# A planner that knows of a shared port: new costs, margins and priorities, and a first batch in chunks of 1, 1, 2 and 2 token tiles

## The chip, the cores and the metric

One core of one Trainium2 chip. The metric is the device time of one execution in microseconds (us), from outside the program; the profile's span is the time from the first to the last instruction of one profiled execution, and is a little shorter.

## The reference

```python
scores = scale * np.matmul(q, k.transpose(0, 1, 3, 2))      # q, k, v: 4 x 8 x 768 x 64
...
scores = np.where(mask, scores, -1000000000.0)
scores = scores - np.max(scores, axis=-1, keepdims=True)
attn = np.exp(scores)
attn = attn / (np.sum(attn, axis=-1, keepdims=True) + 1e-09)
x = np.matmul(attn, v)          # as 3072 x 512: tokens by heads and dims
h = x @ w_in                    # 512 x 2048
g = np.maximum(h, 0.0) + alpha * np.minimum(h, 0.0)
out = g @ w_out                 # 2048 x 512
```

The mask has blocks of 32 tokens: neighbours, the first and last rows and columns, and three drawn blocks for each row. All 768 x 768 scores are computed. The weights arrive as float64.

## The kernel before

Precision: each float32 operand is split into a large float16 part and a small float16 remainder, and a product is three float16 matmuls (large by large, and the two cross terms). So every operand has, besides its own work, a step `hi` (scale and round, line 322 on) and a step `lo` (scale, subtract, lines 330 to 336). On VectorE (DVE) `lo` is one instruction, on GpSimd (POOL) two: a one-input scale (line 335) and a two-input subtraction (line 336). The float64 weights are first made float32 with integer steps on the bits, called n1, n2 and n3 (lines 708, 713 or 715, and 720).

Tiling: a token tile is 128 tokens. A batch has 768 tokens and was cut in three chunks of two tiles (`SIZES0`, and `[2, 2, 2]` for the others). A unit is one chunk and one pair of heads; a step is one token tile of one head, 192 steps in all. This text calls blocks of TensorE (PE) matmuls:
- S block (line 498): the scores of one step, 128 x 768, four matmuls. Then DVE adds the mask and takes the row's extreme (`e`, line 508), ScalarE (ACT) does the exponential (line 515), DVE the reciprocal `rs` (line 523), and P is written as its large part (`ph`, DVE line 327 or ACT line 325) and small part (DVE line 333 or POOL lines 335 and 336). SyncE (SP) transposes P by DMA (line 538).
- A block (line 552): attention times v for one unit, 36 matmuls of 256 columns. Its result `x` is split on ACT and DVE (lines 563 and 568).
- U block (line 852): x by a 256-wide piece of w_in, 24 matmuls of 256 columns, eight for a chunk. Then the activation block on DVE (`g`, lines 862 and 863), the large part `gh` on ACT (line 868) and the small part `gl` on POOL (line 873).
- D block (line 891): g by w_out, 12 matmuls of 512 columns.

U needs x of the chunk's four units and the split w_in; D needs gh, gl and the split w_out. K's scales of all four head pairs of a batch go into `cs`, which every `e` of a later chunk needs; K loads (`kf`) and V loads use the buffers `vf`.

Order: nothing is left to the hardware. The class `Plan` is a list scheduler: each operation has a priority (smaller is earlier; attention step n has about n), costs for the engines that may do it, the operations that it waits for, and buffers to take and free. `run` walks through a model of time, picks an engine for each ready operation, and gives the order in which the kernel is then written; at the end every engine's instructions are chained in that order. Priorities of the weights' steps come from `V_WI`, `W_WI`, `V_WO` and `W_WO`, those of U and D from `MOE_LAG`, and `MOE_BOOST` puts the steps behind U ahead. A cost written as a pair was, for DVE, the time alone and the time while POOL is busy.

Of the kernel before, what the change touches and what calls it, by code (L numbers as in the profile page):

```python
# [23 lines left out]
PSCALE = 2.0**14  # L24
GSCALE = 2.0**-20
SB = 205 << 23
SIZES0 = [2, 2, 2]
MOE_LAG = 11.753
MOE_BOOST = 7.325
V_WI = -10.661  # L30
W_WI = 1.102
V_WO = 12.217
W_WO = 1.038
WI_LO = "pe"
PL_V = -12.594
P_V = -6.546
PL = "ggv"
LD = 4


class Buf:
# [13 lines left out]
class Plan:  # L55
# [2 lines left out]

    ENGINES = ("PE", "DVE", "ACT", "POOL", "SP")
    SHARE = {"SP": 0.3, "ACT": 0.7}  # L60
    LAT = {"PE": 0.15, "DVE": 0.11, "ACT": 0.12, "POOL": 0.08}

    def __init__(self, pools):
        self.ops, self.free = [], dict(pools)
# [11 lines left out]
    def run(self):  # L76
# [31 lines left out]

        def cost(o, e):
            c = o.alts[e]  # L110
            if isinstance(c, tuple):
                c = c[1] if idle["POOL"] > now + 0.2 else c[0]
            return c

        while left:
            progress = True
            while progress:
                progress = False
                ready.sort(key=lambda o: (o.prio, o.n))
                load = dict.fromkeys(self.ENGINES, 0.0)  # L120
                taken = []
                for o in ready:
                    if any(not b.live and self.free[b.pool] <= 0 for b in o.alloc):
                        continue
                    best = min(o.alts, key=lambda e: max(idle[e] - now, 0.0) + load[e] + cost(o, e))
                    if idle[best] > now + 1e-9 or load[best] > 0:
                        load[best] += cost(o, best)
                        continue
                    c = cost(o, best)
                    o.eng, o.start = best, now  # L130
# [12 lines left out]
                    progress = True  # L143
                for o in taken:
                    ready.remove(o)
            both = all(rings.values())
            heads = [(r, self.SHARE[x] if both else 1.0) for x, r in rings.items() if r]
            t_dma = min((now + r[0][0] / w for r, w in heads), default=None)
            t_ev = min((e[0] for e in events), default=None)
            assert t_dma is not None or t_ev is not None, [  # L150
                (o.n, o.prio, o.alts, [(b.pool, self.free[b.pool]) for b in o.alloc]) for o in ready[:12]
            ]
            nxt = min(t for t in (t_dma, t_ev) if t is not None)
            for r, w in heads:
                r[0][0] -= (nxt - now) * w
            now = nxt
            for r, _ in heads:
                if r[0][0] <= 1e-9:
                    events.append((now + 0.9, r[0][1].n, "fin", r[0][1]))
                    r.pop(0)  # L160
            due = sorted(e for e in events if e[0] <= now + 1e-9)
            events = [e for e in events if e[0] > now + 1e-9]
            for _, _, kind, o in due:
                if kind == "dma":
                    rings["SP" if o.eng == "SP" else "ACT"].append([o.dma, o])
                elif kind == "fin":
                    finish(o)
        self.span, self.busy = now, busy
# [4 lines left out]
def attn_moe(ctx: ExitStack, tc: tile.TileContext, q, k, v, sampled, w_in, w_out, alpha, out):  # L173
# [9 lines left out]
    NC = DM // P  # L183
    W2 = 2 * P

    bufs = dict(kt=5, ks=5, v2=5, vf=5, qf=6, qt=3, qn=2, ph=4, e=3, pt=3, x=2, g=3, gh=3, gl=3, junk=2, sid=2)
# [150 lines left out]

    T = {}
    LQ = {"ACT": 0.06}
    MAX4 = {"DVE": (0.55, 1.1), "ACT": 0.85}  # L340
    LOW4 = {"DVE": (0.94, 1.5), "POOL": 2.8}


    steps = [(u, j) for u, (c, hp) in enumerate(units) for j in range(2 * chunks[c][2])]
# [264 lines left out]
    def prep_q(c, prio, pl, gate):  # L609
# [16 lines left out]
        for u, fb in zip(us, fbs):  # L626
            hp = units[u][1]
            p = prio if c == 0 else first[u] - 5
            nb = plan.buf("qn")
            o = plan.op(p, {"POOL": 0.35 + 0.25 * f, "ACT": 0.15 + 0.25 * f, "DVE": (0.1 + 0.15 * f, 0.2 + 0.4 * f)},  # L630
                        lambda e, u=u: emit_q_hi(e, u), [sc[hp]], [nb], [fb])
            o = plan.op(p, {"DVE": (0.14 + 0.27 * f, 0.2 + 0.65 * f)}, lambda u=u: emit_q_lo(u), [o], [], [nb, fb])
            qtbuf[u] = plan.buf("qt")
            o_qt[u] = plan.op(p - 2, {"SP": 0.8 * f}, lambda u=u: emit_q_t(u), [o], [qtbuf[u]], [nb], dma=0.75 * f)

    def attend(n):
# [9 lines left out]
        o = plan.op(n - 2, {"ACT": 0.11}, lambda: emit_dn(n), [o])  # L646
        o = plan.op(n - 2, {"DVE": 0.08}, lambda: emit_rs(n), [o])
        o = plan.op(n - 1, MAX4, lambda e: emit_p_hi(e, n), [o], [pb], [eb])
        lo = {"POOL": 2.8} if PL[n % len(PL)] == "g" else {"DVE": (0.94, 1.5)} if PL[n % len(PL)] == "v" else LOW4
# [6 lines left out]
    def values(u):  # L656
# [8 lines left out]
        o = plan.op(p - 2, {"PE": 0.4 + 1.92 * f}, lambda: emit_av(u), last + [o_v2[b, hp]],  # L665
                    [ab, xbuf[c]], [ptbuf[u, 0], ptbuf[u, 1], vbuf[b, hp]])
        o = plan.op(p - 4, {"ACT": 0.1 + 0.2 * f}, lambda: emit_x_hi(u), [o], [], [ab, xbuf[c]])
        o_x[u] = plan.op(p - 4, {"DVE": 0.1 + 0.25 * f}, lambda: emit_x_lo(u), [o], [], [ab, xbuf[c]])
# [128 lines left out]
    for f in range(NF):  # L797
        p = V_WI + W_WI * f
        o = plan.op(p - 12, LQ, lambda e, f=f: emit_load_w(e, "wi", f, 0), [n3wi[f - 8]] if f >= 8 else [], [plan.buf("ld")], dma=1.6)
        o = plan.op(p, {"DVE": (0.36, 0.6)}, lambda f=f: emit_n1("wi", f, 0), [o])  # L800
        o = plan.op(p, {"ACT": 1.27, "DVE": (0.6, 0.95)}, lambda e, f=f: emit_n2(e, "wi", f, 0), [o])
        n3wi[f] = plan.op(p, {"DVE": (0.61, 0.95)}, lambda f=f: emit_n3("wi", f, 0), [o])
        sqs[f] = plan.op(p, {"ACT": 0.65}, lambda f=f: emit_w_sq("wi", f), [n3wi[f]])
        if f % 2 == 1:
            hb = plan.buf("h")
# [106 lines left out]
    def moe(c):  # L912
# [15 lines left out]
        for i, (kind, j) in enumerate(items):  # L928
            p = start + (stop - start) * i / len(items)
            if kind == "u":  # L930
# [79 lines left out]
```

## Time and profile before

| what | us |
|---|---|
| median of 3 runs (lowest, highest) | 908.3 (907.07, 909.03) |
| the profiled execution | 911.63 |
| its span | 909.9 |
| PE busy | 802.7 (88%) |
| DVE busy | 714.8 (79%) |
| ACT busy | 553.3 (61%) |
| POOL busy | 505.2 (56%) |

How to read the rows that follow. A row of a group has line, engine, operation, out<-in, shape and count, then its busy time in us, the mean ns of one, and the idle time of the engine just before with what ended it. A row of a stretch has, for each engine, the busy us and the count; PEclk is the granted share of PE's clock, DMA the mean busy share of the 16 DMA engines. A row of the timeline has the start, the length and the instructions. A row of a tile's view has the least, the middle and the greatest duration in ns. PEld is PE's loading of the stationary operand, which overlaps its matmuls. A row of the waits has who waited for whom, the sum in us, how often, and the longest. The matmuls' single durations overlap, so blocks are measured from start to start.

### The profile page before, as it was taken

The numbers are of one execution on the slowest core, as the hardware profiler recorded it, in microseconds if no ns is written. First come the engines' busy times: TensorE is split into PE (matmuls) and PEld (weight loads), VectorE is DVE, ScalarE is ACT, GpSimd is POOL, SyncE is SP. The second block draws the span as 40 slices with busy tenths as digits, with TensorE's granted clock in tenths as the row PEclk, the third lists the DMA queues.
The fourth block names the chain that finished last, engine by engine and source line by source line (L and its number), as shares of the span: only waits on it lengthen the run. The fifth ranks groups of instructions, "written<-read, shape, count | busy, mean of one in ns | idle before, by whom it ended". The sixth has DMA issues, their size and how long they took to land.

```text
span 909.9 us, 16946 instructions
## 1 busy us (share of the span) xinstructions
PE 802.7 (88%) x6089; PEld 528.9 (58%) x6089; DVE 714.8 (79%) x1468; ACT 553.3 (61%) x1185; POOL 505.2 (56%) x413
## 2 busy tenths in 40 slices
PE   3757438988888999999989999999989999999998
PEld 1323215646555766666656766566656667666664
DVE  4899999997888898879987877688987887765232
ACT  6697667875755756757566565666566556664111
POOL 3154445775656667566576665456567566555221
PEclk9867767999999999999999999999999999999999
DMA  9997986988997876969976868969976868655000
GB/s 264 288 263 180 203 210 117 185 134 136 170 175 133 156 138 129 210 130 189 202 154 128 128 128 150 189 119 193 187 140 118 156 117 139 116 117 105 1 24 23
DMA packets 393236, 137.45 MB, mean 151 GB/s; under 512 B 355236, under 2 KB 383936, under 8 KB 393152
## 3 DMA queue, kind: packets, MB, share of 16 engines
q1 hardware_dynamic: 354816, 94.41, 60.2%
q10 hardware_dynamic: 38272, 41.95, 16.8%
q8 instruction: 47, 0.77, 0.3%
q14 instruction: 37, 0.30, 0.1%
q0 software_dynamic: 64, 0.02, 0.0%
HBM read 35.67 MB, written 6.29 MB: 46 GB/s over the span
## 4 chain that ended last, share of the span: by engine, by line
DVE 33%; PE 29%; issue 13%; ACT 12%; DMA 5%; POOL 4%; ACTq 2%; POOLq 0%; DVEq 0%
PE h L852 11%; PE o L891 10%; DVE e L508 6%; ACT e L515 5%; PE sp L498 4%; DVE g L862 4%; DVE ph L333 3%; PE av L552 3%; DVE ph L327 3%; ACT ph L325 2%; DVE g L863 2%; ACTq L364 2%; DMA kf<-in_k_dram 2%; DVE wo L720 2%; DVE qn L403 2%
## 5 line engine op out<-in xcount | busy, mean ns | idle before, releaser
L852 PE MATMUL h<-x,wi 128*128 128x256 f16 x2304 | 270.3, 274 | 14.9 <-DVE g L863 14.7
L852 PEld LDWEIGHTS <-wi 128*128 128x128 f16 x2304 | 227.1, 99 | 57.0 <-issue 18.4
L515 ACT ACTIVATE e<-e,nm 128x768 f32<-128x768 f32 x192 | 178.6, 930 | 114.4 <-DVE nm L508 106.7
L891 PE MATMUL o<-wo,gh 128*128 128x512 f16 x768 | 230.8, 382 | 0.0
L336 POOL TENSOR_TENSOR ph<-e,ph 128x768 f16<-128x768 f32 x128 | 216.7, 1693 | 10.7
L873 POOL TENSOR_TENSOR gl<-g,gh 128x512 f16<-128x512 f32 x96 | 119.1, 1241 | 177.8 <-ACT gh L868 173.4
L335 POOL TENSOR_SCALAR e<-e,rs 128x768 f32<-128x768 f32 x128 | 130.2, 1017 | 157.3 <-DVE ph L327 81.2
L508 DVE CUSTOM_DVE_ANT_0 e<-sp,bias,cs 128x768 f32<-128x768 f32 x192 | 191.9, 1008 | 17.0 <-PE sp L498 10.2
L891 PE MATMUL o<-wo,gl 128*128 128x512 f16 x384 | 146.4, 381 | 1.8 <-POOL gl L873 1.8
L868 ACT CAST gh<-g 128x512 f16<-128x512 f32 x96 | 59.1, 616 | 135.4 <-DVE g L863 120.1
L498 PE MATMUL sp<-kt,qt 128*128 128x512 f16 (+1 forms) x384 | 99.1, 341 | 46.7 <-DVE nm L508 46.5
L498 PEld LDWEIGHTS <-qt 128*128 128x128 f16 x768 | 74.4, 101 | 111.3 <-issue 58.4
L325 ACT ACTIVATE ph<-e,rs 128x768 f16<-128x768 f32 x114 | 105.8, 928 | 28.1 <-DVE rs L523 21.5
L891 PEld LDWEIGHTS <-gh 128*128 128x128 f16 x768 | 74.9, 99 | 80.0 <-issue 3.4
L862 DVE TENSOR_SCALAR g<-h,am 128x256 f32<-128x256 f32 x192 | 83.2, 474 | 48.3 <-PE h L852 46.7
L552 PE MATMUL av<-pt,v 128*64 128x256 f16 x1728 | 108.0, 281 | 1.8 <-DMA pt<-ph 1.5
L552 PEld LDWEIGHTS <-v 128*64 128x64 f16 x1728 | 93.6, 113 | 18.8 <-issue 14.7
L498 PE MATMUL sp<-ks,qt 128*128 128x512 f16 (+1 forms) x384 | 99.3, 342 | 0.0
L523 DVE RECIPROCAL rs<-dn 128x1 f32<-128x1 f32 x192 | 29.0, 156 | 76.0 <-ACT dn L519 75.1
L333 DVE SCALAR_TENSOR_TENSOR ph<-e,rs,ph 128x768 f16<-128x768 f32 x64 | 75.2, 1175 | 9.9 <-ACT ph L325 8.6
L863 DVE SCALAR_TENSOR_TENSOR g<-h,gsc,g 128x512 f32<-128x512 f32 x96 | 72.1, 751 | 3.4
L891 PEld LDWEIGHTS <-gl 128*128 128x128 f16 x384 | 37.8, 99 | 49.4 <-POOL gl L873 3.8
(119 smaller groups left out, 734.1 us busy)
## 6 DMA issues: line engine op xcount, KB each, us to landing
wo<-in_moe_w_in_dram ACTq DMA_DIRECT2D x16, 512.0 KB, 6.7
raw<-in_moe_w_out_dram ACTq DMA_DIRECT2D x32, 256.0 KB, 3.8
kf<-in_k_dram ACTq DMA_DIRECT2D x16, 384.0 KB, 4.1
qf<-in_q_dram ACTq DMA_DIRECT2D x48, 128.0 KB, 4.1
ks<-kt SPq DMA_DIRECT2D x32, 192.0 KB, 4.3
vf<-in_v_dram ACTq DMA_DIRECT2D x16, 384.0 KB, 7.6
out_dram<-ob ACTq DMA_DIRECT2D x24, 256.0 KB, 3.5
pt<-ph SPq DMA_TRANSPOSE x192, 4.1
```

Of the source, the lines that this page charges most:

```text
L325: nc.scalar.activation(dst, src, AF.Copy, scale=scale)
L333: nc.vector.scalar_tensor_tensor(dst, src, scale, hi, ALU.mult, ALU.subtract)
L335: nc.gpsimd.tensor_scalar(tmp, src, scale, 1.0, ALU.mult, ALU.mult)
L336: nc.gpsimd.tensor_tensor(dst, tmp, hi, ALU.subtract)
L498: nc.tensor.matmul(T["sp", n][:, a:z], T["qt", u][:, h, i, :], kt[:, h, a:z], start=(x == 0), stop=(x == 1))
L508: nc.vector.tensor_tensor_reduce(T["e", n], T["sp", n], bias[:, t0 + j % w, :], scale=T["cs", c][:, hp : hp + 1], scalar=3.0e38, op0=ALU.a ...
L515: nc.scalar.activation(T["e", n], T["e", n], AF.Exp, bias=T["nm", n], scale=-1.0, accum_out=T["su", n])
L552: nc.tensor.matmul(av[h * D : (h + 1) * D, : n * P], v2[:, h, t, vv, :], T["pt", u, h][:, pl * NT + t, :], start=(m == 0), stop=(m == len( ...
L852: nc.tensor.matmul(ph[:, i, :], win(w, f, ct), x[:, ct, :], start=(m == 0), stop=(m == len(terms) - 1))
L862: nc.vector.tensor_scalar(g[:, i, :], ph[:, i, :], 0.0, am1[:, f : f + 1], ALU.min, ALU.mult)
L873: nc.gpsimd.tensor_tensor(T["gl", c, j], T["g", c, j], T["gh", c, j], ALU.subtract)
L891: nc.tensor.matmul(T["o", c][t], g[:, i, t * P : (t + 1) * P], wout(w, f), start=(f == 0 and m == 0), stop=(f == NF - 1 and m == 2),)
```

## The change

The planner gets a model of the port that DVE and POOL share. A cost written as a pair now has two parts: for POOL the time without the port and then the time with it, for DVE the whole time and 0. A DVE operation with a pair is not started while POOL holds the port, and a POOL operation that begins with it is not started while such a DVE operation runs. All durations are taken longer by a margin (`SLACK`, and 1.15 for DMA), the latencies too. The large part of P may now go to POOL. The first batch is cut in chunks of 1, 1, 2 and 2 token tiles. Priorities and buffer counts are new: `kt`, `ks` and `v2` four for five, `qf` five for six, `qt` two for three; `ph` five for four, and `e`, `pt`, `gh` and `gl` four for three. The diff at its core:

```diff
-SIZES0 = [2, 2, 2]
-MOE_LAG = 11.753
-MOE_BOOST = 7.325
-V_WI = -10.661
...
+SIZES0 = [1, 1, 2, 2]
+MOE_LAG = 11.268
+MOE_BOOST = 1.935
+V_WI = -3.88
+W_WI = 0.209
+V_WO = 4.613
+W_WO = 0.39
...
+BUFS = {"vf": 5, "qf": 5, "qt": 2, "qn": 2, "ph": 5, "e": 4, "pt": 4, "x": 2, "g": 3, "junk": 2, "sid": 2, "kt": 4, "ks": 4, "v2": 4, "gh": 4, "gl": 4}
...
+    SLACK = {"PE": 1.0, "DVE": 1.08, "ACT": 1.05, "POOL": 1.1, "SP": 1.0}
...
         def cost(o, e):
             c = o.alts[e]
-            if isinstance(c, tuple):
-                c = c[1] if idle["POOL"] > now + 0.2 else c[0]
-            return c
+            return self.SLACK[e] * (sum(c) if isinstance(c, tuple) else c)
+
+        def hold(o, e):
+            c = o.alts[e]
+            if not isinstance(c, tuple):
+                return 0.0
+            if e == "DVE":
+                return max(port["to"] - now, 0.0) if port["from"] <= now else 0.0
+            return max(port["dve"] - now, 0.0) if c[0] == 0 else 0.0
...
-                    best = min(o.alts, key=lambda e: max(idle[e] - now, 0.0) + load[e] + cost(o, e))
+                    best = min(o.alts, key=lambda e: max(idle[e] - now, hold(o, e)) + load[e] + cost(o, e))
+                    if hold(o, best) > 1e-9:
+                        continue
...
-    MAX4 = {"DVE": (0.55, 1.1), "ACT": 0.85}
-    LOW4 = {"DVE": (0.94, 1.5), "POOL": 2.8}
+    MAX4 = {"DVE": (0.55, 0), "ACT": 0.85, "POOL": 1.05}
+    LOW4 = {"DVE": (0.94, 0), "POOL": (1.05, 1.65)}
...
-                gl[j] = plan.op(p - MOE_BOOST, {"POOL": 0.2 + 1.1 * f}, lambda j=j: emit_gl(c, j), [o], [lbs[j]], [gb[j], hbs[j]])
+                gl[j] = plan.op(p - MOE_BOOST, {"POOL": (0, 0.1 + 1.08 * f)}, lambda j=j: emit_gl(c, j), [o], [lbs[j]], [gb[j], hbs[j]])
```

The other lines give every cost in the new form and some a new value. What it does to the order shows at three places. DVE before, where the first activation block (`g`) stands; `wo<-raw` is the last n3 of w_out, `x` the last of chunk 0:

```order
L568 SCALAR_TENSOR_TENSOR x<-av,x 128x256
L523 RECIPROCAL rs<-dn 128x1 x2
L720 SCALAR_TENSOR_TENSOR wo<-raw,wo 128x256
L508 ISA e,nm<-sp,bias,cs 128x768
L508 ISA nm 128x1
L333 SCALAR_TENSOR_TENSOR ph<-e,rs,ph 128x768
L746 TENSOR_REDUCE otot<-osum 128x1
L403 SCALAR_TENSOR_TENSOR qn<-qf,sq,qn 128x4x64
L327 TENSOR_SCALAR ph<-e,rs 128x768
L523 RECIPROCAL rs<-dn 128x1
L862 TENSOR_SCALAR g<-h,am_122 128x256 x2
```

DVE at the same place now:

```order
L736 SCALAR_TENSOR_TENSOR wo<-raw,wo 128x256
L343 TENSOR_SCALAR ph<-e,rs 128x768
L584 SCALAR_TENSOR_TENSOR x<-av,x 128x128
L524 ISA e,nm<-sp,bias,cs 128x768
L524 ISA nm 128x1
L762 TENSOR_REDUCE otot<-osum 128x1
L539 RECIPROCAL rs<-dn 128x1
L524 ISA e,nm<-sp,bias,cs 128x768
L524 ISA nm 128x1
L878 TENSOR_SCALAR g<-h,am_122 128x128 x2
```

The last n3 of w_out stands ahead of the last `x` instead of behind it, and the activation block covers 128 tokens; in all 289 instructions stand before it in place of 312, of them 16 `e` in place of 23.

PE before, at the end of the first U block (`h`), where S blocks follow:

```order
L852 MATMUL h<-x,wi 128x256
L852 LDWEIGHTS wi
L852 MATMUL h<-x,wi 128x256
L498 LDWEIGHTS qt
L498 MATMUL sp<-kt,qt 128x512
```

PE at the end of the first U block now:

```order
L868 MATMUL h<-x,wi 128x128
L868 LDWEIGHTS wi
L868 MATMUL h<-x,wi 128x128
L477 MATMUL bc<-ident,otot 128x128
L568 LDWEIGHTS v_664
L568 MATMUL av<-pt,v_664 64x128
```

Each weight load now serves 128 columns in the first two chunks' U and A blocks (16 and 8 short blocks); ahead of the first U stand 16 S and 4 short A blocks, where 24 S and 4 whole A blocks stood, and an A block of chunk 1 follows at once.

ACT before, around the load of batch 1's last K (`kf`); `kss` are its squares:

```order
L364 DMA kf<-in_k_dram 128x2x384
L325 ACTIVATE ph<-e,rs 128x768
L515 ACTIVATE e,su<-e,nm 128x768
L868 CAST gh<-g 128x512
L519 ACTIVATE dn<-su,eps 128x1
L321 ACTIVATE junk,kss<-kf 128x768
```

ACT around the same load now:

```order
L380 DMA kf<-in_k_dram 128x2x384
L884 CAST gh<-g 128x512
L579 ACTIVATE x<-av 128x256
L337 ACTIVATE junk,kss<-kf 128x768
L884 CAST gh<-g 128x512
L531 ACTIVATE e,su<-e,nm 128x768
```

Before, the load is issued behind the 43rd exponential of 192, now behind the 48th, the last of batch 0; two instructions stand between it and the squares, not four, and the next exponential is batch 1's first.

More of the change, by code (lines that the diff above doesn't have):

```diff
@@ L26 @@
 SB = 205 << 23
-SIZES0 = [2, 2, 2]
-MOE_LAG = 11.753
-MOE_BOOST = 7.325
-V_WI = -10.661
-W_WI = 1.102
-V_WO = 12.217
-W_WO = 1.038
+SIZES0 = [1, 1, 2, 2]
[5 more added lines that the diff above has]
+W_WO = 0.39
 WI_LO = "pe"
-PL_V = -12.594
-P_V = -6.546
+PL_V = -3.773
+P_V = -7.4
 PL = "ggv"
 LD = 4
+BUFS = {"vf": 5, "qf": 5, "qt": 2, "qn": 2, "ph": 5, "e": 4, "pt": 4, "x": 2, "g": 3, "junk": 2, "sid": 2, "kt": 4, "ks": 4, "v2": 4, "gh": 4, "gl": 4}
 class Buf:
@@ L60 @@
     SHARE = {"SP": 0.3, "ACT": 0.7}
-    LAT = {"PE": 0.15, "DVE": 0.11, "ACT": 0.12, "POOL": 0.08}
+    LAT = {"PE": 0.2, "DVE": 0.2, "ACT": 0.2, "POOL": 0.15}
+    SLACK = {"PE": 1.0, "DVE": 1.08, "ACT": 1.05, "POOL": 1.1, "SP": 1.0}
     def __init__(self, pools):
@@ L93, in run @@
         order = []
+        port = {"from": 0.0, "to": 0.0, "dve": 0.0}
         busy = dict.fromkeys(self.ENGINES, 0.0)
@@ L129, in run @@
                     c = cost(o, best)
+                    if isinstance(o.alts[best], tuple):
+                        if best == "DVE":
+                            port["dve"] = now + c
+                        else:
+                            port["from"], port["to"] = now + self.SLACK[best] * o.alts[best][0], now + c
                     o.eng, o.start = best, now
@@ L164, in run @@
                 if kind == "dma":
-                    rings["SP" if o.eng == "SP" else "ACT"].append([o.dma, o])
+                    rings["SP" if o.eng == "SP" else "ACT"].append([1.15 * o.dma, o])
                 elif kind == "fin":
@@ L184, in attn_moe @@
     W2 = 2 * P
-    bufs = dict(kt=5, ks=5, v2=5, vf=5, qf=6, qt=3, qn=2, ph=4, e=3, pt=3, x=2, g=3, gh=3, gl=3, junk=2, sid=2)
+    bufs = dict(BUFS)
     cpool = ctx.enter_context(tc.tile_pool(name="const", bufs=1))
@@ L629, in prep_q @@
             nb = plan.buf("qn")
-            o = plan.op(p, {"POOL": 0.35 + 0.25 * f, "ACT": 0.15 + 0.25 * f, "DVE": (0.1 + 0.15 * f, 0.2 + 0.4 * f)},
+            o = plan.op(p, {"POOL": 0.35 + 0.25 * f, "ACT": 0.15 + 0.25 * f, "DVE": (0.1 + 0.15 * f, 0)},
                         lambda e, u=u: emit_q_hi(e, u), [sc[hp]], [nb], [fb])
-            o = plan.op(p, {"DVE": (0.14 + 0.27 * f, 0.2 + 0.65 * f)}, lambda u=u: emit_q_lo(u), [o], [], [nb, fb])
+            o = plan.op(p, {"DVE": (0.14 + 0.27 * f, 0)}, lambda u=u: emit_q_lo(u), [o], [], [nb, fb])
             qtbuf[u] = plan.buf("qt")
@@ L645, in attend @@
         o = plan.op(n - 1, {"ACT": 0.94}, lambda: emit_exp(n), [o], [], [eb])
-        o = plan.op(n - 2, {"ACT": 0.11}, lambda: emit_dn(n), [o])
+        o = plan.op(n - 2, {"ACT": 0.19}, lambda: emit_dn(n), [o])
         o = plan.op(n - 2, {"DVE": 0.08}, lambda: emit_rs(n), [o])
         o = plan.op(n - 1, MAX4, lambda e: emit_p_hi(e, n), [o], [pb], [eb])
-        lo = {"POOL": 2.8} if PL[n % len(PL)] == "g" else {"DVE": (0.94, 1.5)} if PL[n % len(PL)] == "v" else LOW4
+        lo = {"POOL": (1.05, 1.65)} if PL[n % len(PL)] == "g" else {"DVE": (0.94, 0)} if PL[n % len(PL)] == "v" else LOW4
         o = plan.op(n - 1, lo, lambda e: emit_p_lo(e, n), [o], [], [pb, eb])
@@ L664, in values @@
         last = [o_pt[n] for n in range(first[u], first[u + 1])]
-        o = plan.op(p - 2, {"PE": 0.4 + 1.92 * f}, lambda: emit_av(u), last + [o_v2[b, hp]],
+        o = plan.op(p - 2, {"PE": 0.3 + 1.88 * f}, lambda: emit_av(u), last + [o_v2[b, hp]],
                     [ab, xbuf[c]], [ptbuf[u, 0], ptbuf[u, 1], vbuf[b, hp]])
@@ L799, in attn_moe @@
         o = plan.op(p - 12, LQ, lambda e, f=f: emit_load_w(e, "wi", f, 0), [n3wi[f - 8]] if f >= 8 else [], [plan.buf("ld")], dma=1.6)
-        o = plan.op(p, {"DVE": (0.36, 0.6)}, lambda f=f: emit_n1("wi", f, 0), [o])
-        o = plan.op(p, {"ACT": 1.27, "DVE": (0.6, 0.95)}, lambda e, f=f: emit_n2(e, "wi", f, 0), [o])
-        n3wi[f] = plan.op(p, {"DVE": (0.61, 0.95)}, lambda f=f: emit_n3("wi", f, 0), [o])
+        o = plan.op(p, {"DVE": (0.36, 0)}, lambda f=f: emit_n1("wi", f, 0), [o])
+        o = plan.op(p, {"ACT": 1.27, "DVE": (0.6, 0)}, lambda e, f=f: emit_n2(e, "wi", f, 0), [o])
+        n3wi[f] = plan.op(p, {"DVE": (0.61, 0)}, lambda f=f: emit_n3("wi", f, 0), [o])
         sqs[f] = plan.op(p, {"ACT": 0.65}, lambda f=f: emit_w_sq("wi", f), [n3wi[f]])
@@ L811, in attn_moe @@
             for x in (f - 1, f):
-                o = plan.op(p + 0.1, {"ACT": 0.63, "DVE": (0.36, 0.7), "POOL": 0.82}, lambda e, x=x: emit_w_hi(e, "wi", x), [gs[-1], prev])
+                o = plan.op(p + 0.1, {"ACT": 0.63, "DVE": (0.36, 0), "POOL": 0.82}, lambda e, x=x: emit_w_hi(e, "wi", x), [gs[-1], prev])
                 if WI_LO == "pe":
@@ L817, in attn_moe @@
                 else:
-                    prev = o_wi[x] = plan.op(p, {"DVE": (0.67, 1.1), "POOL": 2.3}, lambda e, x=x: emit_w_lo(e, "wi", x), [o], [], [sb])
+                    prev = o_wi[x] = plan.op(p, {"DVE": (0.67, 0), "POOL": (0.8, 1.25)}, lambda e, x=x: emit_w_lo(e, "wi", x), [o], [], [sb])
     o_gsc = plan.op(V_WI + W_WI * NF - 2, {"DVE": 0.5}, emit_gsc, gs + [o_al])
@@ L828, in attn_moe @@
             o = plan.op(p - 8 + 0.1 * h, LQ, lambda e, f=f, h=h: emit_load_w(e, "wo", f, h), [n3wi[min(NF - 1, 8 + f // 2)]], [rb, plan.buf("ld")], dma=0.8)
-            o = plan.op(p, {"DVE": (0.22, 0.6)}, lambda f=f, h=h: emit_n1("wo", f, h), [o] + free, [], [rb])
-            o = plan.op(p, {"ACT": 0.7, "DVE": (0.34, 0.5)}, lambda e, f=f, h=h: emit_n2(e, "wo", f, h), [o], [], [rb])
-            n3.append(plan.op(p, {"DVE": (0.34, 0.5)}, lambda f=f, h=h: emit_n3("wo", f, h), [o], [], [rb]))
+            o = plan.op(p, {"DVE": (0.22, 0)}, lambda f=f, h=h: emit_n1("wo", f, h), [o] + free, [], [rb])
+            o = plan.op(p, {"ACT": 0.7, "DVE": (0.34, 0)}, lambda e, f=f, h=h: emit_n2(e, "wo", f, h), [o], [], [rb])
+            n3.append(plan.op(p, {"DVE": (0.34, 0)}, lambda f=f, h=h: emit_n3("wo", f, h), [o], [], [rb]))
         osq.append(plan.op(p, {"ACT": 0.65}, lambda f=f: emit_w_sq("wo", f), n3))
@@ L839, in attn_moe @@
     for f in range(NF):
-        o = plan.op(p + 0.1 * f, {"ACT": 0.63, "DVE": (0.36, 0.7), "POOL": 0.82}, lambda e, f=f: emit_w_hi(e, "wo", f), [o_swo, prev])
-        prev = o_wo[f] = plan.op(p + 0.1 * f, {"DVE": (0.67, 1.1), "POOL": 2.3}, lambda e, f=f: emit_w_lo(e, "wo", f), [o])
+        o = plan.op(p + 0.1 * f, {"ACT": 0.63, "DVE": (0.36, 0), "POOL": 0.82}, lambda e, f=f: emit_w_hi(e, "wo", f), [o_swo, prev])
+        prev = o_wo[f] = plan.op(p + 0.1 * f, {"DVE": (0.67, 0), "POOL": (0.8, 1.25)}, lambda e, f=f: emit_w_lo(e, "wo", f), [o])
     def emit_up(c, j):
```

## The prediction

> **What bounds the kernel now.** I read the page first, then the busy time by stretches, then the waits and the order of each engine in the stretches that are not full.
>
> ```profile
> span 909.9 us, 16946 instructions
> ```
>
> ```profile
> core 0: us, PE busy (x) PEld busy (x) DVE busy (x) ACT busy (x) POOL busy (x), PEclk, DMA share, GB/s
> 0.00:18.00 18.00, 3.92 (x14) 2.70 (x15) 6.46 (x36) 9.73 (x23) 6.91 (x23) 1.00 0.95 272
> 18.00:146.80 128.80, 75.92 (x334) 38.09 (x333) 118.94 (x264) 97.00 (x219) 53.69 (x43) 0.73 0.91 218
> 146.80:355.00 208.20, 191.31 (x1528) 128.45 (x1527) 184.34 (x356) 135.82 (x290) 137.57 (x108) 0.98 0.85 150
> 355.00:700.00 345.00, 326.07 (x2603) 220.26 (x2603) 282.86 (x571) 219.54 (x470) 209.58 (x161) 1.00 0.85 158
> 700.00:909.90 209.90, 205.43 (x1622) 139.42 (x1616) 122.20 (x247) 91.21 (x184) 97.44 (x79) 1.00 0.47 89
> ```
>
> I cut at 146.8 us because the first U block starts there. Up to it DVE is busy 118.94 of 128.8 us and PE 75.92, at a granted clock of 0.73: the head belongs to DVE, which splits the weights. From then on PE is the bound: it idles 16.9, 18.9 and 4.5 us in the three stretches, 40.3 of 763. So the time is the start of the first U, plus PE's work behind it, plus PE's idle time behind it, and I price the change in these three.
>
> PE's blocks, in the timeline of PE:
>
> ```profile
> 146.79 4.33 PE L852 MATMUL h<-x,wi 128*128 128x256 f16 x24
> ...
> 155.60 2.15 PE L552 MATMUL av<-pt,v 128*64 128x256 f16 x36
> 157.69 0.50 PE L498 MATMUL sp<-kt,qt 128*128 128x512 f16 x2
> ...
> 158.35 0.49 PE L498 MATMUL sp<-kt,qt 128*128 128x512 f16 x2
> ...
> 166.36 2.78 PE L852 MATMUL h<-x,wi 128*128 128x256 f16 x24
> 168.98 0.49 PE L498 MATMUL sp<-kt,qt 128*128 128x512 f16 x2
> ```
>
> From start to start an A block takes 2.09 us (155.60 to 157.69), an S block 0.66, a U block 2.62, which is 109 ns for each of its 24 matmuls.
>
> **The head: fewer instructions ahead of the first U.** Up to the first activation block DVE has in the new order 16 `e` in place of 23, 6 large parts of P for 9 and 4 small ones for 7, one `qn` of 256 columns and 8 of 128 for ten of 256, and 5 more n2 instructions for `wo`. DVE's groups from 0 to 152 us price them:
>
> ```profile
> L720 DVE SCALAR_TENSOR_TENSOR wo<-raw,wo 128x256 int32<-128x256 int32 x32 | 23.4, 751 | 1.5 <-ACT raw L713 1.3
> L508 DVE CUSTOM_DVE_ANT_0 e<-sp,bias,cs 128x768 f32<-128x768 f32 x23 | 22.9, 1006 | 3.5 <-PE sp L498 3.5
> ...
> L327 DVE TENSOR_SCALAR ph<-e,rs 128x768 f16<-128x768 f32 x9 | 8.2, 915 | 0.0
> L715 DVE SCALAR_TENSOR_TENSOR wo<-raw,wo 128x256 int32<-128x256 int32 x17 | 8.0, 486 | 0.0
> L333 DVE SCALAR_TENSOR_TENSOR ph<-e,rs,ph 128x768 f16<-128x768 f32 x7 | 7.6, 1089 | 0.0
> ...
> L403 DVE SCALAR_TENSOR_TENSOR qn<-qf,sq,qn 128x256 f16<-128x256 f32 x10 | 4.7, 473 | 0.0
> ```
>
> That is -7 x 1.006 - 3 x 0.915 - 3 x 1.089 = -13.0; `qn` -9 x 0.473 + 8 x 0.3 = -1.9 (no short one is in the trace; 0.3 is an estimate between half and the whole of 0.473); n2 +5 x 0.486 = +2.4. Sum **-12.5 us**; single differences of under 2 us, of both signs, are left out. DVE is 92% busy here, so I take it whole.
>
> **The head: the port.** Two pairs from the timeline around 187 us:
>
> ```profile
> 186.45 0.74 DVE L333 SCALAR_TENSOR_TENSOR wo<-wo,s_wo 128x512 f16<-128x512 f32 x1
> 186.58 1.39 POOL L335 TENSOR_SCALAR e<-e,rs 128x768 f32<-128x768 f32 x1 [2.22 <-ACT ph L325]
> ...
> 188.06 1.69 POOL L336 TENSOR_TENSOR ph<-e,ph 128x768 f16<-128x768 f32 x1
> 188.16 2.13 DVE L333 SCALAR_TENSOR_TENSOR wo<-wo,s_wo 128x512 f16<-128x512 f32 x1
> ```
>
> Beside POOL's one-input step the DVE instruction takes 0.74 us; started just behind POOL's two-input step it takes 2.13, that is, it waits for POOL's end at 189.75 and then runs. That is what the new planner models: only POOL's two-input instructions hold the port. The Trainium skill (SBUF — State Buffer, "SBUF: two separate sides") calls the shared pair an exclusive lock taken by any GpSimd op that reads SBUF, one input or two, against a DVE op in a 2-port mode or with two SBUF inputs; the second pair agrees, the first does not. By that rule the 31 large parts of P that move to POOL, one-input steps, could hold DVE up by as much as 31 x 1.39 = 43 us, spread over the run; by the row they do not, and I charge nothing for them.
>
> How much waiting is in the head: the means above against the medians in the views by tile, `wo` to 220 us and `ph` over the run.
>
> ```profile
> L720 DVE SCALAR_TENSOR_TENSOR wo<-raw,wo x32: 396/414/1871, 75.6 to 147.9; 128x256 int32<-128x256 int32 x32
> ```
>
> ```profile
> L327 DVE TENSOR_SCALAR ph<-e,rs x78: 600/620/1993, 55.3 to 827.7; 128x768 f16<-128x768 f32 x78
> ```
>
> 32 x (0.751 - 0.414) + 9 x (0.915 - 0.620) = 10.8 + 2.7 = 13.5 us in these two groups. The order fixes only what follows what on one engine; how DVE and POOL lie against each other slips by a microsecond or so, which is as long as these instructions. So between 0 and 13.5 I take somewhat under half, **-6 us**. Head together -18: first U at about 129 us.
>
> DMA, 0.91 busy in the head (117 us), does not stop this: all weights are loaded as before, but 8 fewer P transposes precede the first U, and the transposes' queue says what they are worth.
>
> ```profile
> q1 hardware_dynamic: 354816, 94.41, 60.2%
> ```
>
> 0.602 x 909.9 / 192 is at most 2.9 us each, up to 23 us of DMA that leaves the head. If the loads did land late all the same, the first U would come as late as they do.
>
> **PE's work behind the first U.** Before it stand 16 S blocks in place of 24, and 4 short A blocks in place of 4 whole ones. So 8 S blocks move behind it, +8 x 0.66 = 5.3; 4 short A blocks are added there; and 16 short U blocks stand for 8 whole ones. (D blocks keep their matmuls.) No short block is in the trace. PE's weight loads bound it:
>
> ```profile
> L852 PEld LDWEIGHTS <-wi 128*128 128x128 f16 x2304 | 227.1, 99 | 57.0 <-issue 18.4
> L552 PEld LDWEIGHTS <-v 128*64 128x64 f16 x1728 | 93.6, 113 | 18.8 <-issue 14.7 <-DMA pt<-ph 2.5 <-DMA qt<-qn 0.2
> ```
>
> A short U takes half of 2.62, 1.31 us, if only columns count, and 24 x 0.099 = 2.37 if a load of 99 ns must end before the next begins; between them 1.85. That is 16 x 1.85 - 8 x 2.62 = +8.6 (0 to +16.9). A short A lies between 1.05 and 2.09, I take 1.6: +6.3 (4.2 to 8.4). Together **+20 us** (9.5 to 30.6). The Trainium skill (TensorE: Matmul & The Clock Gate, "Back-to-back issue gap") gives about 81 ns per matmul at 128 columns in a stream of load and matmul, which speaks against this change; by it, as an estimate, a short U is 1.94 us and the sum 1.5 us more.
>
> **PE's idle time behind the first U.** Who it waits for, 146.8 to 355 and then 350 to 910:
>
> ```profile
> PE sp L498 <- DVE nm L508: 10.9, 10, 3.5
> PE h L852 <- DVE g L863: 3.6, 3, 2.5
> ```
>
> ```profile
> PE h L852 <- DVE g L863: 11.0, 10, 2.1
> ```
>
> Most of what has a releaser is DVE coming late. DVE loses 30 large parts of P to POOL (78 to 48; 30 x 0.620 = 18.6 us) and some waits at the port, which in the whole run are worth 78 x (0.827 - 0.620) = 16 us for this group alone:
>
> ```profile
> L327 DVE TENSOR_SCALAR ph<-e,rs 128x768 f16<-128x768 f32 x78 | 64.3, 827 | 1.1
> ```
>
> Against it, the short chunks put DVE's work closer together just behind the first U. The last 4.5 us, the output's way out, stay. From 40.3 I take **-13** (0 to -30).
>
> The sum: 909.9 - 12.5 - 6 + 20 - 13 is about 898.5, that is 11 us less. The profiled execution took 911.6 in all, the median of the runs is 908.3, 3.3 less; so 908.3 - 11 = **897**. What is late next: PE everywhere, then K's loads.
>
> **The rivals.** *The short matmuls eat the gain* (slower): in the stretch of the 16 short U blocks DVE is full too, so idle time does not shrink, and if a short U takes x, the change is -18 + 5.3 + 6.3 + 16x - 21. It turns at x = 1.71 us, 71 ns per matmul; at 1.94 it is +4, at 2.37 with long A blocks +12.6: 912 to 921, I say 916. For it: 99 ns loads. Against it: PE has idle time there that longer blocks partly fill. Chance 0.2.
>
> *K's load comes late.* Batch 1's fourth K load is issued at exponential 48 in place of 43, and only two ACT instructions stand between it and its squares; the scales of the next chunk need all four. Landings of K around 180 to 260 us:
>
> ```profile
> DMA to landing us min/median/max: 3.2/3.8/9.3
> ```
>
> At 9.3 in place of 3.8, ACT and the chunk's scores wait 5.5 us, and at the next two batches perhaps again: 903 to 908. For it: that 9.3 occurred in before. Against it: PE has U and D blocks queued. Chance 0.1.
>
> *The holds do not reach the chip*: the alignment slips, no wait at the port goes, and idle time shrinks by half as much: -12.5 + 20 - 6.5 = +1, no change, 904 to 911. Chance 0.15.
>
> *The port works fully*: all of the 13.5 us, idle down by 25: -12.5 - 13.5 + 20 - 25 = -31, 877. Chance 0.1.
>
> My forecast, 885 to 904, has 0.45. Beyond about 0.2% (906.5 to 910.1) a measurement of this kernel can tell a difference. Faster: 0.45 + 0.1, most of K's case, a third of the holds' case, 0.67; same 0.12; slower 0.21. The range 882 to 915 leaves out most of the port's full case and half of the short matmuls'.
>
> **What would show it.** First `h` matmul at 127 to 132 us, not 147; 16 short U blocks of 1.85 us start to start (under 1.5 or over 2.2 refutes the term); PE idle behind the first U near 27 us; mean of DVE's `ph` toward 0.7 us; no gap of PE at exponential 48. A first U after 138 us, or idle time above 40 us, would make the forecast wrong.

## The result, and the profile after

| | before | changed |
|---|---|---|
| median of 4 runs (lowest, highest), us | 907.68 (905.49, 909.03) | 880.99 (879.48, 882.39) |
| span of the profiled execution, us | 909.9 | 877.7 |

The ratio is 0.9708, 95% interval 0.9681 to 0.9734: 27 us faster. The forecast was 897 with a range from 882 to 915: the direction held, the time lies 1 us below the range, and the gain was more than twice the 11 us that I gave. The two profiled executions took 911.6 and 879.5 us, so their spans differ by 5.5 us more than the medians.

The changed kernel by stretches, cut at its own first U block:

```profile
0.00:18.00 18.00, 3.84 (x13) 2.61 (x14) 7.70 (x37) 8.37 (x22) 7.33 (x23) 1.00 0.89 265
18.00:130.10 112.10, 60.71 (x302) 30.16 (x301) 102.30 (x245) 77.67 (x186) 37.99 (x31) 0.72 0.90 215
130.10:355.00 224.90, 211.84 (x1979) 147.69 (x1978) 204.81 (x426) 161.79 (x362) 175.23 (x138) 0.99 0.95 166
355.00:700.00 345.00, 341.81 (x2795) 233.72 (x2793) 292.02 (x587) 228.52 (x497) 235.50 (x187) 1.00 0.89 165
700.00:877.70 177.70, 173.25 (x1343) 117.22 (x1340) 100.89 (x194) 68.42 (x135) 82.89 (x68) 1.00 0.43 81
```

The first figure behind the length of a stretch is PE's busy time. The first U starts at 130.1 us, 16.7 earlier. Behind it PE works 726.9 us (722.8 before) and idles 13.1 + 3.2 + 4.5 = 20.7 (40.3 before). -16.7 + 4.1 - 19.6 = -32.2 is the whole difference of the two spans. From 355 to 700 us PE's idle time fell from 18.9 to 3.2 us.

The short blocks in PE's timeline:

```profile
148.91 1.20 PE L568 MATMUL av<-pt,v 128*64 128x128 f16 x36
150.04 0.50 PE L514 MATMUL sp<-kt,qt 128*128 128x512 f16 x2
...
154.28 1.50 PE L868 MATMUL h<-x,wi 128*128 128x128 f16 x24 [0.23 <-DVE g L879]
155.61 0.49 PE L514 MATMUL sp<-kt,qt 128*128 128x512 f16 x2
```

Start to start a short U takes 1.33 us, 55 ns per matmul, and a short A 1.13: half of the long ones (2.62 and 2.09) plus 0.02 and 0.08.

DVE's parts of P, large and small:

```profile
L349 DVE SCALAR_TENSOR_TENSOR ph<-e,rs,ph 128x768 f16<-128x768 f32 x64 | 83.6, 1306 | 2.9 <-ACT ph L341 2.8
L343 DVE TENSOR_SCALAR ph<-e,rs 128x768 f16<-128x768 f32 x48 | 48.3, 1006 | 1.2 <-DVE rs L539 0.3
```

The large part took 827 ns on average before, now 1006, with a median still at 0.62 us: per instruction DVE waits more at the port, not less. Sorted by what POOL did when they started, the 18 with POOL idle throughout took 0.62 us in the median, the 7 that started during a one-input step 0.99, the 16 during a two-input step 1.62. Over all steps of DVE, the time above what the same step takes undisturbed (the shortest tenth of its group) is 109.5 us before and 109.2 now: the waits at the port did not go. What became rarer is something else. DVE's own waits from 355 to 700 us, before:

```profile
DVE rs L523 <- ACT dn L519: 39.0, 32, 3.0
```

And after:

```profile
DVE e L524 <- PE sp L514: 13.0, 15, 1.7
DVE g L878 <- PE h L868: 11.8, 14, 1.5
DVE rs L539 <- ACT dn L535: 9.8, 12, 2.5
```

Before, DVE stood 39 us in front of a reciprocal `rs` whose operand `dn` ACT had not yet written, with everything behind it in its queue waiting as well. During 20 of these 39 us ACT was still at the exponential, during 9 at `dn` itself. Now DVE waits mostly for PE, which is what an engine off the bound should wait for.

How such a wait reaches PE, in before's timelines of ACT, DVE and PE:

```profile
539.12 0.94 ACT L515 ACTIVATE e<-e,nm 128x768 f32<-128x768 f32 x1 [1.97 <-DVE nm L508]
539.96 0.19 ACT L515 ACTIVATION_READ_ACCUMULATOR e<-e,nm 128x1 f32 x1
540.18 0.29 ACT L519 ACTIVATE dn<-su,eps 128x1 f32<-128x1 f32 x1
...
540.51 0.16 DVE L523 RECIPROCAL rs<-dn 128x1 f32<-128x1 f32 x1 [1.43 <-ACT dn L519]
540.59 0.86 DVE L862 TENSOR_SCALAR g<-h,am 128x256 f32<-128x256 f32 x2
541.48 0.75 DVE L863 SCALAR_TENSOR_TENSOR g<-h,gsc,g 128x512 f32<-128x512 f32 x1
...
542.29 1.47 PE L852 MATMUL h<-x,wi 128*128 128x256 f16 x12 [0.42 <-DVE g L863]
```

DVE waits 1.43 us for `dn`, the activation block stands behind the reciprocal, and the next U block waits for it: `h` has one buffer in PSUM, the memory that matmuls write.

DVE can also be late by the port. Just ahead of PE's longest wait in this stretch, 2.13 us from 475.4 on, before's DVE timeline has:

```profile
470.81 1.64 DVE L390 TENSOR_SCALAR cs<-cs 128x4 f32<-128x4 f32 x1
472.36 1.20 DVE L327 TENSOR_SCALAR qn<-qf,sq 128x256 f16<-128x256 f32 x2
473.48 1.93 DVE L403 SCALAR_TENSOR_TENSOR qn<-qf,sq,qn 128x256 f16<-128x256 f32 x1
...
475.80 0.86 DVE L862 TENSOR_SCALAR g<-h,am 128x256 f32<-128x256 f32 x2
476.69 0.75 DVE L863 SCALAR_TENSOR_TENSOR g<-h,gsc,g 128x512 f32<-128x512 f32 x1
```

A step on four columns, 0.17 us when POOL is idle, takes 1.64 us behind a two-input step of POOL that started at 470.78, and the next splits run late; the activation block behind them ends at 477.4, and the next U block starts at 477.50.

Between 355 and 700 us PE waited 14 times for 0.3 us or more until DVE had done a step, 14.2 us in all. Ahead of ten of these waits, 9.0 us, DVE had stood over 1 us in front of `rs` within the last 6 us. Ahead of the other four, 5.2 us, it had not, but its steps had been lengthened by 0.9 to 2.1 us. In the changed kernel five such waits are left, 2.9 us, none of them behind an `rs` wait of 1 us.

### The profile page after: what moved, and what is told of

It reads as the page before. It is cut to its first block, busy times and chain, and to the rows that moved or that the text cites. A ratio compares the mean times of both kernels' runs of the same rounds, so it can differ in the third digit from the quotient of the medians.

```text
span 877.7 us, 17627 instructions
## 1 busy us (share of the span) xinstructions
PE 791.4 (90%) x6425; PEld 531.4 (61%) x6425; DVE 707.7 (81%) x1487; ACT 544.8 (62%) x1199; POOL 538.9 (61%) x445
## 4 chain that ended last, share of the span: by engine, by line
PE 59%; DVE 17%; issue 7%; POOL 3%; ACT 2%; DMA 2%; POOLq 0%; ACTq 0%; DVEq 0%
PE h L868 21%; PE o L907 20%; PE sp L514 9%; PE av L568 8%; DVE e L524 4%; DVE ph L349 2%; DVE g L878 2%; DVE wo L349 1%; DVE qn L419 1%; POOL gl L889 1%; DVE g L879 1%; DMA raw<-in_moe_w_out_dram 1%; DVE kn L349 1%; DVE wo L736 1%; DMA kt<-kn 1%
## 5 line engine op out<-in xcount | busy, mean ns | idle before, releaser
L868 PE MATMUL h<-x,wi 128*128 128x256 f16 (+1 forms) x2496 | 270.6, 265 | 7.1 <-DVE g L879 6.1
L868 PEld LDWEIGHTS <-wi 128*128 128x128 f16 x2496 | 230.1, 98 | 46.2 <-issue 11.2
L352 POOL TENSOR_TENSOR ph<-e,ph 128x768 f16<-128x768 f32 x128 | 221.9, 1734 | 10.7
L889 POOL TENSOR_TENSOR gl<-g,gh 128x512 f16<-128x512 f32 (+1 forms) x104 | 121.3, 1168 | 128.8 <-ACT gh L884 124.6
L351 POOL TENSOR_SCALAR e<-e,rs 128x768 f32<-128x768 f32 x128 | 132.6, 1036 | 104.7 <-ACT ph L341 49.7
L884 ACT CAST gh<-g 128x512 f16<-128x512 f32 (+1 forms) x104 | 60.4, 581 | 143.3 <-DVE g L879 136.5
L878 DVE TENSOR_SCALAR g<-h,am 128x256 f32<-128x256 f32 (+1 forms) x208 | 86.1, 454 | 65.9 <-PE h L868 65.6
L514 PE MATMUL sp<-kt,qt 128*128 128x512 f16 (+1 forms) x384 | 98.1, 338 | 26.3 <-DVE nm L524 20.7
L568 PE MATMUL av<-pt,v 128*64 128x256 f16 (+1 forms) x1872 | 108.2, 273 | 10.2 <-DVE x L584 10.2
L349 DVE SCALAR_TENSOR_TENSOR ph<-e,rs,ph 128x768 f16<-128x768 f32 x64 | 83.6, 1306 | 2.9 <-ACT ph L341 2.8
L879 DVE SCALAR_TENSOR_TENSOR g<-h,gsc,g 128x512 f32<-128x512 f32 (+1 forms) x104 | 73.8, 710 | 3.7
L535 ACT ACTIVATE dn<-su,eps 128x1 f32<-128x1 f32 x192 | 53.8, 287 | 4.6 <-ACT e L531 1.7
```

What stands on the lines that cost most here:

```text
L349: nc.vector.scalar_tensor_tensor(dst, src, scale, hi, ALU.mult, ALU.subtract)
L351: nc.gpsimd.tensor_scalar(tmp, src, scale, 1.0, ALU.mult, ALU.mult)
L352: nc.gpsimd.tensor_tensor(dst, tmp, hi, ALU.subtract)
L514: nc.tensor.matmul(T["sp", n][:, a:z], T["qt", u][:, h, i, :], kt[:, h, a:z], start=(x == 0), stop=(x == 1))
L568: nc.tensor.matmul(av[h * D : (h + 1) * D, : n * P], v2[:, h, t, vv, :], T["pt", u, h][:, pl * NT + t, :], start=(m == 0), stop=(m == len( ...
L868: nc.tensor.matmul(ph[:, i, :], win(w, f, ct), x[:, ct, :], start=(m == 0), stop=(m == len(terms) - 1))
```

## The experiments

Theories at the outset. *Slack*: margins and buffers let attention run ahead, so a late DVE step no longer reaches PE. *Port*: the holds do it. *Relief*: P's large parts on POOL do it. *Head*: the short chunks do it. Every variant but the one with split U blocks makes the planner write a new order, so two controls come first. The priorities stay as they are in the kernel that a variant starts from; they were not chosen anew for any variant, so a part of a loss may be priorities that no longer fit. Ratios are to the kernel before, with 95% intervals; the changed kernel has 0.971.

**Controls.** `MOE_LAG = 11.35` for 11.268; and `V_WI = -3.8` for -3.88.

> A control: the changed kernel with MOE_LAG 11.35 for 11.268, less than a tenth of an attention step, so the planner makes another order by the same model. If single undoings can be read as the price of what they undo: within 0.004 of 0.971. If an order of this planner is one draw among many, and the changed one a chosen one: 0.975 to 0.995.

> A second control: the changed kernel with V_WI -3.80 for -3.88. Readings as for the first control: within 0.004 of 0.971, or 0.975 to 0.995.

Measured: 0.9667 (0.9638 to 0.9696) and 0.9678 (0.9644 to 0.9712). These two new orders by the same model are within about 0.004 of 0.971, so an undoing that moves clearly more can be read.

**The price of short matmuls**, in the kernel before:

```diff
+            for z in range(n):
                 for m, (w, x, ct) in enumerate(terms):
-                    ph[:, i, :], win(w, f, ct), x[:, ct, :], ...
+                    ph[:, i, z * P : (z + 1) * P], win(w, f, ct), x[:, ct, z * P : (z + 1) * P], ...
```

> The kernel before with every U matmul of 256 columns written as two of 128, so 2304 more weight loads and matmuls in the same planned order. At 56 ns per matmul, as the short U blocks of the changed kernel show, a U block stays at about 2.7 us and the time at 1.000 to 1.012. At 81 ns a U block takes 3.9 us and the time grows by up to 122 us, to 1.10 or more; at 99 ns more still.

Measured: 0.9989 (0.9964 to 1.0014), at the cheap end. All U blocks split, PE's matmuls and weight loads by group:

```profile
L853 PE MATMUL h<-x,wi 128*128 128x128 f16 x4608 | 276.9, 220 | 14.6 <-DVE g L865 13.0 <-DVE ku L313 1.3 <-DVE x L568 0.2
```

```profile
L853 PEld LDWEIGHTS <-wi 128*128 128x128 f16 x4608 | 267.6, 99 | 32.2 <-DVE g L865 19.9 <-issue 1.0
```

276.9 / 4608 is 60 ns per matmul. A load still lasts 99 ns, but 4608 of them cover only 267.6 us, 58 each: loads overlap one another. Short U blocks are nearly free.

**The changed kernel with one part undone.** No holds: `hold` returns 0.

> The changed kernel whose planner never holds an operation back for the port; all else stays. Theory slack (the gain behind the first U comes from margins and more buffers, which let attention run ahead of PE's need): 0.968 to 0.978 of before, PE idle behind the first U 18 to 26 us, for the waits at the port in the trace of the changed kernel are no fewer than before. Rival port (the holds bring it): 0.985 or more, idle behind the first U above 32 us.

Measured: 1.0154 (1.0128 to 1.018), PE idle behind the first U 49.7 us in the longest of its five executions. My expectation failed, and the rival's range was met. DVE's steps are now lengthened by 139.7 us in place of 109.2; from 355 to 700 us PE waited seven times for DVE, 12.3 us in all, never behind a wait for `rs`, but each time behind 1.0 to 2.8 us of lengthened steps. But this planner has no price for the port left at all. So the holds were replaced by the old second values (`{"DVE": (0.55, 1.1)}` and so on, taken while POOL is busy):

> The changed kernel in which only the port's handling is the old one: no operation is held back, and a DVE step with a pair costs its old second value while POOL is busy; margins, buffers, sizes, priorities stay. If the holds themselves are what the planner gained: 0.990 or more, idle behind the first U above 35 us. If it was only fatal to ignore the port (the kernel without holds had no price for it at all), and the old price does as well: 0.968 to 0.980.

Measured: 0.9754 (0.9726 to 0.9783), the second reading: 887.7 us, where the controls beside it took 880.2 and 880.8. The holds are worth about 7 us over the old price; to leave the port out costs 40. The 7 us are not fewer waits at the port: DVE's steps are lengthened by 104.5 us here.

No margins (`SLACK` 1, old `LAT`, DMA factor 1.0), and each of the three alone:

> The changed kernel without margins: SLACK all 1, the old latencies, DMA times 1.0; buffers, port, sizes and priorities as changed. Theory slack, with the margins as its main part: 0.982 to 0.992, idle behind the first U 30 us or more. Rival buffers (the extra buffers do it): within 0.004 of the changed kernel's 0.971.

> The changed kernel with SLACK 1 for all engines, latencies and DMA margin kept. If the durations' margin is the part that counts of the 0.044 that the three margins together were worth: 0.990 or more. If it is the latencies or the DMA times: under 0.980.

> The changed kernel with the old latencies (0.08 to 0.15 us) in place of 0.15 to 0.2; SLACK and DMA margin kept. If the latencies are what keeps a DVE step from standing in the queue ahead of its operand: 0.980 or more, rs waiting 20 us or more for dn from 355 to 700 us (9.8 in the changed kernel). If SLACK covers it: 0.968 to 0.976.

> The changed kernel with DMA times taken as they were (factor 1.0 for 1.15). If late transfers are what the margins guard against: 0.980 or more, with PE or ACT waiting for loads or P transposes. Else 0.968 to 0.976.

Measured: 1.0152 (1.0109 to 1.0196); without SLACK 1.0024 (0.9992 to 1.0057), with old latencies 0.9893 (0.9806 to 0.998), without DMA's margin 0.9783 (0.9719 to 0.9846). All margins gone cost more than I expected, and buffers without margins keep nothing of the gain; the first of the readings held for SLACK and for the latencies, neither of the two for DMA's margin. SLACK counts most. DVE's wait without SLACK and with the old latencies, 355 to 700 us:

```profile
DVE rs L539 <- ACT dn L535: 20.6, 21, 2.0
```

```profile
DVE rs L539 <- ACT dn L535: 29.0, 24, 3.5
```

Both are over twice the 9.8 us of the changed kernel. But the longer wait goes with the shorter time, so the waits for `rs` are not the whole of what the margins mend.

Old buffers, no large parts on POOL, old sizes, old `MOE_LAG` and `MOE_BOOST`:

> The changed kernel with the old buffer counts. Rival buffers: 0.982 or more, idle behind the first U above 30 us, with PE waiting for DVE's nm and g again. If margins alone do it: 0.968 to 0.976.

> The changed kernel in which P's large part may not go to POOL. Rival relief (DVE's 30 moved instructions, 18.6 us, are what PE no longer waits for): 0.978 to 0.988. Theory slack: DVE is 85% busy from 355 to 700 us and PE waits little, so 0.969 to 0.976.

> The changed kernel with the first batch in chunks of 2, 2, 2. Theory head (8 steps of attention ahead of the first U in place of 16 bring 10 us or more): first U at 140 to 148 us, 0.980 to 0.988. Rival (the weights' priorities bring the head): first U before 135 us, 0.969 to 0.976.

> The changed kernel with the old MOE_LAG and MOE_BOOST (11.753 and 7.325): activation blocks rank ahead of attention again. If the place of the activation blocks is what keeps PE fed: 0.980 or more and PE waiting for nm. Theory slack: 0.968 to 0.977.

Measured: 0.9952 (0.9928 to 0.9976), 0.9803 (0.9767 to 0.984), 0.984 (0.9797 to 0.9884), 0.9912 (0.9874 to 0.9949). The range of rival buffers was met, with PE idle for 44.5 us behind the first U. Slack's forecasts failed for the parts on POOL, where relief's range was met, and for `MOE_LAG` and `MOE_BOOST`: each of the four counts for something. With the old sizes the time is in the range of theory head, but the first U came at 164.9 us, not at 140 to 148: 35 us later than in the changed kernel, for 12 us of time, since PE did more attention first and idled only 12.6 us behind it.

**The kernel before with parts added.** Sizes and weight priorities; buffers and margins; each alone:

> The kernel before with the new SIZES0 and the new priorities of weights and V alone; old costs, buffers, no margins. Theory head: first U at 128 to 136 us, idle behind it still 35 us or more, 0.982 to 0.992.

> The kernel before with the new buffer counts and the margins alone; sizes, priorities and the port's handling as before. Theory slack (margins and buffers bring the gain behind the first U): idle behind the first U 20 to 28 us in place of 40, 0.975 to 0.988. If they work only together with priorities chosen for them: 0.995 or more.

> The kernel before with the new buffer counts alone. If the buffers bring most of what buffers and margins together brought (0.976): 0.985 or less, PE idle from 355 to 700 us under 10 us in place of 18.9. If the margins do: 0.993 or more, idle there 14 us or more.

> The kernel before with the margins alone (SLACK, latencies, DMA times). If the margins bring most of it: 0.985 or less, PE idle from 355 to 700 us under 10 us, and DVE's wait of rs for dn there, 39 us before, under 20. If the buffers do: 0.993 or more.

Measured: 1.0144 (1.0102 to 1.0186); **0.9763 (0.9722 to 0.9803)** for both; buffers alone 1.0178 (1.0109 to 1.0246), margins alone 0.996 (0.9926 to 0.9995). The sizes without margins lose, against my forecast, although the first U comes at 118.5 us. Buffers and margins bring 0.024 together and next to nothing or less apart, so neither single reading held. With the margins alone PE's idle time behind the first U falls to 21.8 us, but the first U comes only at 170.2; with both it comes at 158.6, and PE idles 16.6 us behind it. The new counts are not all larger: five kinds of buffers have one more, `kt`, `ks`, `v2`, `qf` and `qt` one fewer, and which of them lose alone was not tried. DVE's wait and PE's busy time, 355 to 700 us, with both:

```profile
DVE rs L524 <- ACT dn L520: 13.8, 15, 2.4
```

```profile
355.00:700.00 345.00, 341.35 (x2779) 233.64 (x2778) 303.49 (x595) 231.53 (x497) 225.60 (x171) 1.00 0.91 166
```

With the buffers alone:

```profile
DVE rs L523 <- ACT dn L519: 35.6, 33, 3.4
```

```profile
355.00:700.00 345.00, 327.56 (x2620) 222.02 (x2620) 293.53 (x574) 208.48 (x456) 213.92 (x163) 0.99 0.82 154
```

PE idles 3.7 us with both, 17.4 with the buffers alone. Yet with the buffers alone only 2 of the 14 waits of PE for DVE in this stretch, 1.2 of 15.2 us, stand behind an `rs` wait of over 1 us.

Over the kernels of this document the two go together: PE idles 13 to 19 us from 355 to 700 us where DVE waits 33 to 39 us for `rs` there (before, split U, sizes, buffers alone), and 2.4 to 6.6 where it waits under 14, save without the holds, where it idles 14.7. That the one makes the other is shown for single waits only.

**What the margins mend.** The planner's costs against the trace of before: dn 0.11 for 0.288 us, the exponential 0.94 for 0.930 and 0.187 for its sum. Buffers with true costs for five steps, no margin:

```diff
...
-        o = plan.op(n - 1, {"ACT": 0.94}, lambda: emit_exp(n), [o], [], [eb])
-        o = plan.op(n - 2, {"ACT": 0.11}, lambda: emit_dn(n), [o])
-        o = plan.op(n - 2, {"DVE": 0.08}, lambda: emit_rs(n), [o])
...
+        o = plan.op(n - 1, {"ACT": 1.12}, lambda: emit_exp(n), [o], [], [eb])
+        o = plan.op(n - 2, {"ACT": 0.29}, lambda: emit_dn(n), [o])
+        o = plan.op(n - 2, {"DVE": 0.16}, lambda: emit_rs(n), [o])
...
```

> The kernel before with the new buffer counts and, in place of any margin, the durations that its trace shows for five steps whose costs were too small: exponential 1.12 for 0.94 us (0.930 and 0.187 for its sum), dn 0.29 for 0.11, e 1.09 for 0.94, rs 0.16 for 0.08, the activation block 1.7 for 1.46. If the margins mend these costs: 0.975 to 0.988, with DVE's wait of rs for dn from 150 to 800 us under 35 us (56 with the buffers alone). If a margin on everything is needed, for steps that slip against each other: 1.000 or more.

Measured: 0.9893 (0.9849 to 0.9936), 0.001 beyond the first range and far from the second; `rs` waits 17.6 us from 150 to 800 us, as the first reading wanted. DVE's wait, 355 to 700 us:

```profile
DVE rs L523 <- ACT dn L519: 9.5, 8, 2.0
```

From 1.0178 to 0.9893 is 0.0285, two thirds of the 0.0415 that the margins bring on top of the buffers. So five costs put right are worth two thirds of the margins, but not by the same way: the first U comes at 132.0 us here and PE idles 35.6 us behind it, at 158.6 and 16.6 with the margins.

## Why the prediction was wrong, step by step

- *The head, -18 us*: the first U was forecast at 129 and came at 130.1. The count of instructions held. DVE's busy time to the first U fell by 15.4 us; of these, 6.4 are steps lengthened less beside POOL (22.9 us before, 16.5 now; forecast 6), so the fewer instructions brought about 9, not 12.5. The port's share is plain for the last step of w_out's bits alone: 506 ns on average to 130 us in place of 751. But an early first U is no gain by itself. It came at 118.5 in a kernel that is slower than before and at 164.9 in one of 0.984, since attention that is not done ahead of the first U must be done behind it.
- *PE's work behind the first U, +20 us*: measured +4.1, below even the low end of 9.5. This term failed. With 16 us it is most of the 20.7 by which the sum missed the difference of the two spans (-11.5 for -32.2). I put a short U halfway between half a long one and a row of weight loads at 99 ns each; it took 1.33 us, the lower end, for the loads overlap. By line, U's busy time behind the first U grew by 0.3 us (forecast 8.6), A's by 5.4 (6.3), S's by 3.9 (5.3), and D's, forecast as unchanged, fell by 2.1; matmuls of different lines overlap, so these do not add up to 4.1. So half of the 16 us is the pace of the loads, and the rest is small pieces. The mean duration of a load was read as its pace. In U's own row before, 227.1 us for 2304 loads, the two are the same; but the row for A's loads beside it, 93.6 us for 1728 loads of 113 ns, is 54 ns each and shows loads that overlap. The Trainium skill's 81 ns (TensorE: Matmul & The Clock Gate, "Back-to-back issue gap") does not hold here either, 55 to 60 ns do; that section's figure for an isolated matmul, about 56 ns, is the one that fits.
- *PE's idle time, -13 us*: measured -19.6. The size was near, the reason was not. I named the parts of P that moved to POOL and shorter waits at the port. The moved parts are worth about 0.01; the waits per instruction grew. Margins and buffers, which I did not price at all, carry most of it: together, on the kernel before, they bring 0.024 of 0.029 and PE's idle time from 40.3 to 16.6 us. They are enough there, but not the only condition: in the changed kernel a planner without any price for the port loses as much as one without margins.
- *Only two-input steps hold the port*: this reading of the first pair was wrong. There DVE had started at 186.45, before POOL at 186.58, so it had nothing to wait for, and it is POOL's step that is longer, 1.39 us in place of 0.91. A few rows on in the same timeline the same DVE step starts behind a one-input step:

```profile
191.29 0.90 POOL L335 TENSOR_SCALAR e<-e,rs 128x768 f32<-128x768 f32 x1
...
191.48 1.25 DVE L333 SCALAR_TENSOR_TENSOR wo<-wo,s_wo 128x512 f16<-128x512 f32 x1
```

It waits for POOL's end at 192.19 and runs 0.54 us on, as in the second pair. So one-input steps hold DVE up too, as in the rule of the Trainium skill that the prediction quotes and sets aside, and the new planner's model of the port leaves them out. DVE steps that started during one were lengthened by 21.1 us before and 30.0 now. To charge nothing for the moved parts was luck: the 31 of them held DVE up only four times, 2.3 us.

- *The rivals*: short matmuls eat the gain, refuted. K's load comes late: its landings from 200 to 270 us took at most 4.9 us, and PE did not wait for a norm of K there. The holds do not reach the chip: half right. The planner kept DVE off POOL's two-input steps in its model, and still 75 DVE steps were lengthened behind one, by 0.9 us on average; yet PE's idle time halved, and the holds are worth 7 us. The port works fully, 877: close in time, by another mechanism.

What stays open: the parts do not add up (undone one by one in the changed kernel they cost 0.5 to 4.5% each, where the whole change is worth 2.9%), so no share can be given to each. Why the buffers alone lose 1.8% is not shown: few of PE's waits there stand behind a wait for `rs`. What the last third of the margins' effect is was not tried. Nor was a planner that counts POOL's one-input steps as holding the port.

## What to carry to other kernels

Where a planner writes the order of in-order queues, a step that is placed ahead of its operand holds up all that stands behind it, here 39 us in 345: check each cost against the trace, and try margins and buffers together, since here neither paid alone. Do not price a schedule by when its main phase starts; work that is moved out of the head comes back behind it. Read an overlapped engine's pace from busy time by count, not from a mean duration, and in a row where the engine is pressed. And before two rows are read as who waits for whom, look which of them started first.

## What the runs showed of the hardware

- Weight loads of 128 x 128 float16 last 99 ns and yet, with matmuls of 128 columns, 4608 of them cover only 58 ns each; these matmuls run at 55 to 60 ns. With matmuls of 256 columns the loads cover 99 ns each (227.1 us for 2304).
- A GpSimd step held up VectorE steps that read four columns or more from SBUF, whether it had two inputs or one: a step on four columns, 0.17 us alone, took 1.64 us behind a two-input step (470.8 us in before) and 0.85 behind a one-input step (469.9). Who starts first matters: the VectorE step at 186.45 us, begun 0.13 us before GpSimd's, took its usual 0.74. Where GpSimd's step had itself begun during a VectorE step, the next VectorE step sometimes went ahead of it (0.41 us, as alone, at 112.16 us in before).
- Not held up were steps that read their scores from PSUM, and the reciprocals on one column: all 192 `e` of the kernel before took 0.99 to 1.02 us, 111 of them begun while a GpSimd step ran, and all 192 `rs` 0.13 to 0.17 us.
- ScalarE's `dn` on one column takes 288 ns, and the read of the accumulator behind each exponential 187 ns; the planner had 0.11 us for the one and nothing for the other.
